# Retention and two feed-forward layers on one core: weight loads two pairs ahead, and the last chunk stored by halves

## The chip, the cores and the metric

The kernel runs on one core of a Trainium2 chip. The metric is the device time of one execution, in microseconds (us). TensorE (PE) multiplies matrices, PEld is its weight load, VectorE (DVE) and ScalarE (ACT) work elementwise, GpSimd (POOL) scales a few operands, and SyncE (SP) issues every DMA transfer of this kernel, in program order, on one queue.

## The reference, cut to what matters

```python
# B, H, S, D = 4, 8, 576, 64
scores = q @ k.T / sqrt(D)
ret = (scores * Dmat) @ v          # Dmat[h, i, j] = gamma[h]**(i - j) where i >= j, else 0
x = ret.transpose(0, 2, 1, 3).reshape(B * S, H * D)          # 2304 x 512
g = x @ w_gate;  x = (g * sigmoid(g) * (x @ w_val)) @ w_out  # inner size 1536
r = max(x @ w_in, 0);  out = (r * r) @ w_out2                # inner size 2048
```

q, k and v are 32-bit floats. The five weight matrices are 64-bit floats.

## The kernel before, in words

**Attention, the first 128 us.** There are 16 pairs, each a batch and two heads. The loop at L515 has one turn n per pair and two more, because the second half of a pair (`apply`) runs two turns late (LAG = 2). A turn issues `load_kv(n+1)` and `load_qk(n+2)` on SP, then on PE `scores(n)` for four row blocks, `apply(n-2)` into the bank `o`, `scores` for the fifth block, `states(n)` into the bank `kvs`, and the fifth block of `apply(n-2)`, which writes into the bank of `scores(n)` behind the columns that VectorE reads for `pl`. VectorE masks the scores into `p_sb` and `pl` and carries the state `sb`. ScalarE copies `o` into the activations `xy`, and scales the keys of the next pair in `prep_state` (`kv_sb<-kv_sb,ks_sb`). In turns 3 to 6 `split_x` splits a quarter of the first 512 tokens of `xy` into `xh` (fp32r) and the rest `xl`. From turn 6 on `hidden1_early` computes one gate or value block of the first token chunk in each turn, 12 matmuls of 128x512 in a bank `g` or `v`. qk_p has three buffers and kv_p four, so a load waits until the pair that held its buffer is done.

**Weights.** A unit is a 128x512 block of a weight matrix. `prefetch` loads it as 128x1024 words into `raw` (512 KB), from a pool of two buffers, or into a `spare` area. The generator `conversion` (L161) turns a unit into fp32 in five steps: ScalarE takes the low and the high words (`raw<-raw`, `w<-raw`), VectorE clamps, shifts, merges and adds (the add is the row `CUSTOM_DVE_ANT_0`, printed as `ISA` in the order of instructions). In the third step of the next unit `parts_unit` splits it into `w_hi` (ScalarE) and `w_lo` (VectorE). `pump` runs so many steps at given places of the loops. While the attention runs, every instruction is chained to the one before it on its engine, so the order in the code is the order on the engine.

The line that starts the conversion in turn 3 (FROM is 6) is

```python
            if n == FROM - 3:
                prefetch(1)
            if new:
                scores(n, range(NC - 1))
            pump(fill if n == FROM - 3 else 2 * fill)
```

and from there on a turn advances one unit. UNITS_EARLY = 15 units are meant to be converted in the attention. Their parts live in a pool of WA = 21 pairs of tiles.

**The seam and after.** After turn 17 `split_x` splits the second token chunk. Then come the steps of the first layer and of the second one: `hidden1` (24 matmuls) and `out1` (12 matmuls, into four banks `a`) for each of 12 blocks f, and `hidden2` and `out2` for 16 blocks, for five token chunks. Every product has three matmuls: hi by hi, hi by lo, lo by hi. Right behind the seam stand `hidden1` of chunk 1 and six `out1` of chunk 0 (the early blocks), which need the units 12 to 17. Behind the attention the order is not chained but left to a scheduler. The last chunk of the second layer has 256 tokens, two banks `a`; `out2` copies one with ScalarE and one with VectorE into `o_sb` and stores each with one transfer (L366 to L371).

Of the kernel before, what the change touches and what calls it, by code (L numbers as in the profile page):

```python
# [9 lines left out]
F32 = mybir.dt.float32  # L10
# [4 lines left out]
ALU = mybir.AluOpType  # L15
# [4 lines left out]
DM = H * D  # L20
NT = B * S
P = 128
CC = DM // P
F1 = 1536 // P
F2 = 2048 // P
NC = -(-S // P)
N = 512
CHUNKS = {
    1: [(0, 512), (512, 512), (1024, 256), (1280, 512), (1792, 512)],
    2: [(0, 512), (512, 512), (1280, 512), (1792, 512), (1024, 256)],  # L30
}
NCH = len(CHUNKS[1])
# [4 lines left out]
FROM = 6  # L37

LAG = 2

WA = 21

WARM = 4
UNITS_EARLY = WA - HALF

PUMPS = {0: 1, 1: 4, 2: 1}
# [9 lines left out]
def retention_moe_kernel(  # L56
# [56 lines left out]
    pe, dve, act, pool_e, sp = map(Chained, (nc.tensor, nc.vector, nc.scalar, nc.gpsimd, nc.sync))  # L113
# [6 lines left out]
    raw_t, raw_flat, w_t = {}, {}, {}  # L120
    spare = []
# [82 lines left out]
    def pump(k=1):  # L204
        for _ in range(k):
            if pumped["n"] < pumped["limit"]:
                pumped["n"] += 1
                next(convert, None)
# [144 lines left out]
    def out2(n, f):  # L353
        if f == 0:
            acc[2, n] = accs(CHUNKS[2][n][1] // P)
        h = hs.pop((2, n, f))
        ensure((2, "o", f))
        w = units[2, "o", f]
        for tt in range(CHUNKS[2][n][1] // P):
            three(acc[2, n][tt], cut(h, tt * P, P), w, f == 0, f == F2 - 1)  # L360
        if f == F2 - 1:
            for tt, a in enumerate(acc.pop((2, n))):
                if tt % 2 == 0:
                    o = raw_p.tile([P, 1024], U32, tag="raw", name="o_sb").bitcast(F32)
                t = o[:, (tt % 2) * 512:][:, :512]
                if tt % 2:  # L366
                    dve.tensor_copy(t, a)
                else:
                    act.copy(t, a)
                r0 = CHUNKS[2][n][0] + tt * P  # L370
                sp.dma_start(out=out[r0:r0 + P, :], in_=t)  # L371


# [2 lines left out]
    with ExitStack() as st:  # L376
        const = pool(st, "const", 1)
# [9 lines left out]
        rs = [slice(h * D, (h + 1) * D) for h in range(2)]  # L387
        pairs = [(b, hp) for b in range(B) for hp in range(NP)]

        def warm():  # L390

            one = const.tile([P, 256], F32, tag="one", name="one")
            dve.memset(one, 1.0)
            ps = bank("g")
            for _ in range(WARM):
                pe.matmul(ps[:, :256], one[:, :P], one, start=True, stop=True)

        def load_qk(n):
# [7 lines left out]
        def load_kv(n):  # L406
            b, hp = pairs[n]
            kv_t[n] = kv_p.tile([P, 2 * NC - 1, P], F32, tag="kv", name="kv_sb")
            sp.dma_start(out=kv_t[n], in_=kv[b, hp])
            if n < NP:  # L410
                sp.dma_start(out=mask_sb[:, n], in_=mask[:, n])
                sp.dma_start(out=qs_sb[:, n], in_=qscale[:, n, P:P + qs_sb.shape[-1]])

        def prep_state(n):
            hp = pairs[n][1]
            for h, r in enumerate(rs):
                kn = kv_t[n][:, NC:, r]
                act.mul(kn, kn, ks_sb[:, hp, 1, h])
            qs = q_p.tile([P, S - P], F32, tag="qs", name="qs")
            for c, m in ((0, 3 * P), (3 * P, D)):  # L420
                w = min(m, P)
                pool_e.tensor_tensor(
                    out=qs[:, c:c + m].rearrange("p (c q) -> p c q", q=w),
                    in0=qk_t[n][:, 0, P + c:P + c + m].rearrange("p (c q) -> p c q", q=w),
                    in1=qs_sb[:, hp, None, :w].to_broadcast([P, m // w, w]), op=ALU.mult,
                )
            q_t[n] = qs
# [73 lines left out]
            act.copy(xy[:, hp, t0:t0 + bank.shape[-1]], bank)  # L501

        chain["on"] = True
        warm()
        mask_sb = const.tile([P, NP, 2, P], F32, tag="mask", name="mask_sb")
        ks_sb = const.tile([P, NP, NC - 1, 2, 1], F32, tag="ks", name="ks_sb")

# [4 lines left out]
        prep_state(0)  # L512
        last = len(pairs) - 1
        pumped["limit"] = 5 * UNITS_EARLY
        for n in range(last + 1 + LAG):  # L515
            new, old, nxt = n <= last, n >= LAG, n + 1 <= last
            fill = PUMPS[0] if n >= FROM - 3 else 0
            if nxt:
                load_kv(n + 1)
            if n + 2 <= last:  # L520
                load_qk(n + 2)
            if n == FROM - 3:
                prefetch(1)
            if new:
                scores(n, range(NC - 1))
            pump(fill if n == FROM - 3 else 2 * fill)
            if old:
                apply(n - LAG, False)
            pump(fill)
            if LAG < n <= LAG + CC:  # L530
                split_x(1, 0, n - LAG - 1)
            if new:
                scores(n, (NC - 1,))
            pump(fill)
            if new:
                states(n)
            pump(fill)
            if FROM <= n < FROM + 2 * HALF:
                hidden1_early(n - FROM)
            if old:  # L540
                apply(n - LAG, True)
            if nxt:
                prep_state(n + 1)
        for cc in range(CC):
            split_x(1, 1, cc)
    chain["on"] = False


# [98 lines left out]
```

## Time and profile before

| | |
|---|---|
| median of three runs | 943.98 us (943.98 to 945.04) |
| the profiled execution's own time | 942.15 us |
| its span | 940.4 us |
| mean granted TensorE clock, as a share of 2.4 GHz | 0.991 |
| PE busy | 920.8 us (98%) |
| DVE, ACT, POOL busy | 466.3, 340.9, 21.3 us |
| HBM read, written | 56.44 MB, 5.77 MB |

The times of the parts below are those of the profiled execution, counted from the start of its span. A row of the timeline gives start, duration, engine, operation, output<-input and the number of merged instructions; what stands in brackets is the idle time before it and what ended that. All rows carry L106, a helper through which the engines are called, so they are told apart by their tiles.

### The profile page before, as it was taken

Reading aid. Unit: us, or ns where it says so; the run is one execution under the profiler, and the core shown is the slowest. Engines: PE = TensorE matmul, PEld = TensorE weight load, DVE = VectorE, ACT = ScalarE, POOL = GpSimd, SP = SyncE. Lnnn points to the kernel's source line nnn. Section 1 sums busy time; section 2 is a strip of 40 time slices with the busy share of each in tenths; the row PEclk is TensorE's granted clock in tenths of the full one; section 3 lists DMA queues with packets and bytes.
Section 4 is the critical chain, followed back from the end, with each engine's and each line's share of the span. In section 5 each row is a group of like instructions: output and inputs, shape, how many; then the busy total and the mean of one; then the engine's idle time right before and its main releaser. Section 6 shows DMA issues by size and latency. Waiting matters only on the chain.

```text
span 940.4 us, 12525 instructions
## 1 busy us (share of the span) xinstructions
PE 920.8 (98%) x5144; PEld 769.6 (82%) x5144; DVE 466.3 (50%) x845; ACT 340.9 (36%) x629; POOL 21.3 (2%) x39
## 2 busy tenths in 40 slices
PE   8699999999999999999999999999999999999998
PEld 6577778878889998888888888888888888888896
DVE  3688778797424242223899886242224223322332
ACT  2465565554312121112665664232223223222222
POOL 2111100000000000000000000000000000000000
PEclk8799999999999999999999999999999999999999
DMA  8676453542100000001244420000001000100000
GB/s 309 211 249 238 153 157 113 153 137 68 45 1 1 1 2 0 1 1 45 88 136 135 135 90 1 0 34 13 1 1 45 0 1 1 45 1 0 15 31 23
DMA packets 22024, 63.01 MB, mean 67 GB/s; under 512 B 2256, under 2 KB 3792, under 8 KB 21968
## 3 DMA queue, kind: packets, MB, share of 16 engines
q1 hardware_dynamic: 21968, 62.22, 19.6%
q8 instruction: 40, 0.66, 0.3%
q14 instruction: 16, 0.13, 0.0%
HBM read 56.44 MB, written 5.77 MB: 66 GB/s over the span
## 4 chain that ended last, share of the span: by engine, by line
PE 88%; DMA 5%; DVE 4%; ACT 2%; issue 1%; SPq 0%; ACTq 0%
PE a L106 33%; PE g L106 24%; PE v L106 24%; DMA raw<-in_w 3%; PE s L106 3%; PE o L106 3%; DVE w L106 2%; PE kvs L106 1%; DMA xy<-in_w 1%; DVE w_lo L106 1%; DVE t L106 1%; DMA kv_sb<-in_kv 0%; ACT raw L106 0%; DMA part<-part_sb 0%; DVE xl L106 0%
## 5 line engine op out<-in xcount | busy, mean ns | idle before, releaser
L106 ACT ACTIVATE t<-g 128x512 f32<-128x512 f32 (+1 forms) x100 | 55.4, 554 | 211.8 <-PE g L106 211.6
L106 ACT CAST h_hi<-t 128x512 fp32r<-128x512 f32 (+1 forms) x134 | 77.1, 575 | 119.2 <-DVE t L106 113.6
L106 DVE TENSOR_TENSOR h_lo<-t,h_hi 128x512 fp32r<-128x512 f32 (+1 forms) x134 | 85.2, 636 | 67.1 <-ACT h_hi L106 66.7
L106 PE MATMUL v<-xh,w_hi 128*128 128x512 f32 (+1 forms) x304 | 113.8, 374 | 0.0
L106 PE MATMUL g<-xh,w_hi 128*128 128x512 f32 (+1 forms) x304 | 113.8, 374 | 0.0
L106 PE MATMUL g<-xh,w_lo 128*128 128x512 f32 (+1 forms) x304 | 113.3, 373 | 0.0
L106 PE MATMUL v<-xh,w_lo 128*128 128x512 f32 (+1 forms) x304 | 113.2, 373 | 0.0
L106 PE MATMUL g<-xl,w_hi 128*128 128x512 f32 (+1 forms) x304 | 113.2, 372 | 0.0
L106 PE MATMUL v<-xl,w_hi 128*128 128x512 f32 (+1 forms) x304 | 113.2, 372 | 0.0
L106 PE MATMUL a<-w_lo,h_hi 128*128 128x512 f32 x288 | 112.3, 390 | 0.0
L106 PE MATMUL a<-w_hi,h_hi 128*128 128x512 f32 x288 | 112.2, 390 | 0.0
L106 PE MATMUL a<-w_hi,h_lo 128*128 128x512 f32 x288 | 110.1, 389 | 0.0
L106 DVE TENSOR_TENSOR t<-g,t 128x512 f32<-128x512 f32 (+1 forms) x60 | 38.2, 636 | 89.7 <-ACT t L106 89.6
L106 PE MATMUL a<-h_lo,w_hi 128*128 128x512 f32 (+1 forms) x216 | 79.0, 366 | 0.5 <-DVE h_lo L106 0.5
L106 PE MATMUL a<-h_hi,w_lo 128*128 128x512 f32 (+1 forms) x216 | 78.9, 366 | 0.0
L106 DVE SCALAR_TENSOR_TENSOR t<-g,t 128x512 f32<-128x512 f32 (+1 forms) x40 | 25.5, 639 | 105.6 <-ACT t L106 105.4
L106 PE MATMUL a<-h_hi,w_hi 128*128 128x512 f32 (+1 forms) x216 | 76.8, 367 | 0.1
L106 DVE SCALAR_TENSOR_TENSOR t<-v,t 128x512 f32<-128x512 f32 (+1 forms) x40 | 25.6, 639 | 91.7 <-ACT t L106 91.4
L106 DVE TENSOR_SCALAR w<-w 128x512 f32<-128x512 f32 (+1 forms) x136 | 57.4, 423 | 25.9 <-ACT w L106 24.4
L106 PEld LDWEIGHTS g<-xh,w_hi 128*128 128x128 f32 x304 | 57.3, 188 | 10.4 <-issue 0.2
L106 PEld LDWEIGHTS v<-xh,w_hi 128*128 128x128 f32 x304 | 57.3, 188 | 10.2 <-issue 0.2
L106 PEld LDWEIGHTS v<-xh,w_lo 128*128 128x128 f32 x304 | 57.3, 188 | 10.1
(81 smaller groups left out, 1477.6 us busy)
## 6 DMA issues: line engine op xcount, KB each, us to landing
raw<-in_w SPq DMA_DIRECT2D x51, 512.0 KB, 3.6
kv_sb<-in_kv SPq DMA_DIRECT2D x16, 576.0 KB, 4.0
xy<-in_w SPq DMA_DIRECT2D x17, 512.0 KB, 3.7
qk_sb<-in_qk SPq DMA_DIRECT2D x15, 576.0 KB, 5.1
out<-o_sb SPq DMA_DIRECT2D x18, 256.0 KB, 2.2
part<-part_sb SPq DMA_DIRECT2D x4, 256.0 KB, 2.9
xy<-part SPq DMA_DIRECT2D x1, 1024.0 KB, 5.2
mask_sb<-in_mask SPq DMA_DIRECT2D x4, 128.0 KB, 7.3
```

What stands on the lines that cost most here:

```text
L106: i = op(*args, **kw)
```

## The change

It changes six things.

- The first two weight loads are issued in turn 2 instead of 3 (`FROM - 4`), the conversion starts in turn 4 instead of 3 (`FROM - 2`), and a third load buffer, `raw3`, joins the two of the pool while the attention runs. 14 units instead of 15 are converted there (WA = 20). The loads of the loop stop at unit 13 and are all taken up when it ends: one more step of conversion is pumped, and the third buffer is given up.
- In turn 17 the fifth block of `apply` comes ahead of `hidden1_early`.
- The load of the first keys and values is cut in two, keys first, and one of the two scalings of these keys goes from ScalarE to VectorE.
- Of four warming matmuls at the start three stay there and two more stand behind the first scores.
- `out2` of the last chunk copies the left half of each bank with ScalarE and the right half with VectorE, and stores each half with a transfer of its own: four of 128 KB instead of two of 256 KB.
- WA being one less, the pool of the later weight tiles has one more pair.

```diff
--- before.py
+++ after.py
@@ -38,9 +38,9 @@
 
 LAG = 2
 
-WA = 21
-
-WARM = 4
+WA = 20
+
+WARM = 3
 UNITS_EARLY = WA - HALF
 
 PUMPS = {0: 1, 1: 4, 2: 1}
@@ -363,11 +363,17 @@
                 if tt % 2 == 0:
                     o = raw_p.tile([P, 1024], U32, tag="raw", name="o_sb").bitcast(F32)
                 t = o[:, (tt % 2) * 512:][:, :512]
+                r0 = CHUNKS[2][n][0] + tt * P
+                if n == NCH - 1:
+                    for x, copy in enumerate((act.copy, dve.tensor_copy)):
+                        at = slice(x * (DM // 2), (x + 1) * (DM // 2))
+                        copy(t[:, at], a[:, at])
+                        sp.dma_start(out=out[r0:r0 + P, at], in_=t[:, at])
+                    continue
                 if tt % 2:
                     dve.tensor_copy(t, a)
                 else:
                     act.copy(t, a)
-                r0 = CHUNKS[2][n][0] + tt * P
                 sp.dma_start(out=out[r0:r0 + P, :], in_=t)
 
 
@@ -387,12 +393,10 @@
         rs = [slice(h * D, (h + 1) * D) for h in range(2)]
         pairs = [(b, hp) for b in range(B) for hp in range(NP)]
 
-        def warm():
-
-            one = const.tile([P, 256], F32, tag="one", name="one")
-            dve.memset(one, 1.0)
+        def warm(k):
+
             ps = bank("g")
-            for _ in range(WARM):
+            for _ in range(k):
                 pe.matmul(ps[:, :256], one[:, :P], one, start=True, stop=True)
 
         def load_qk(n):
@@ -406,7 +410,8 @@
         def load_kv(n):
             b, hp = pairs[n]
             kv_t[n] = kv_p.tile([P, 2 * NC - 1, P], F32, tag="kv", name="kv_sb")
-            sp.dma_start(out=kv_t[n], in_=kv[b, hp])
+            for at in (slice(NC, 2 * NC - 1), slice(0, NC)) if n == 0 else (slice(0, 2 * NC - 1),):
+                sp.dma_start(out=kv_t[n][:, at], in_=kv[b, hp][:, at])
             if n < NP:
                 sp.dma_start(out=mask_sb[:, n], in_=mask[:, n])
                 sp.dma_start(out=qs_sb[:, n], in_=qscale[:, n, P:P + qs_sb.shape[-1]])
@@ -415,7 +420,10 @@
             hp = pairs[n][1]
             for h, r in enumerate(rs):
                 kn = kv_t[n][:, NC:, r]
-                act.mul(kn, kn, ks_sb[:, hp, 1, h])
+                if n or h:
+                    act.mul(kn, kn, ks_sb[:, hp, 1, h])
+                else:
+                    dve.tensor_scalar(out=kn, in0=kn, scalar1=ks_sb[:, hp, 1, h], scalar2=None, op0=ALU.mult)
             qs = q_p.tile([P, S - P], F32, tag="qs", name="qs")
             for c, m in ((0, 3 * P), (3 * P, D)):
                 w = min(m, P)
@@ -501,7 +509,9 @@
             act.copy(xy[:, hp, t0:t0 + bank.shape[-1]], bank)
 
         chain["on"] = True
-        warm()
+        one = const.tile([P, 256], F32, tag="one", name="one")
+        dve.memset(one, 1.0)
+        warm(WARM)
         mask_sb = const.tile([P, NP, 2, P], F32, tag="mask", name="mask_sb")
         ks_sb = const.tile([P, NP, NC - 1, 2, 1], F32, tag="ks", name="ks_sb")
 
@@ -512,18 +522,22 @@
         prep_state(0)
         last = len(pairs) - 1
         pumped["limit"] = 5 * UNITS_EARLY
+        loads["cap"], loads["open"] = UNITS_EARLY - 1, True
+        spare.append(const.tile([P, 2, 512], F32, tag="raw3", name="raw3"))
         for n in range(last + 1 + LAG):
             new, old, nxt = n <= last, n >= LAG, n + 1 <= last
-            fill = PUMPS[0] if n >= FROM - 3 else 0
+            fill = PUMPS[0] if n >= FROM - 2 else 0
             if nxt:
                 load_kv(n + 1)
             if n + 2 <= last:
                 load_qk(n + 2)
-            if n == FROM - 3:
+            if n == FROM - 4:
                 prefetch(1)
             if new:
                 scores(n, range(NC - 1))
-            pump(fill if n == FROM - 3 else 2 * fill)
+            if n == 0:
+                warm(2)
+            pump(fill if n == FROM - 2 else 2 * fill)
             if old:
                 apply(n - LAG, False)
             pump(fill)
@@ -535,14 +549,20 @@
             if new:
                 states(n)
             pump(fill)
+            if n == last + LAG:
+                apply(n - LAG, True)
             if FROM <= n < FROM + 2 * HALF:
                 hidden1_early(n - FROM)
-            if old:
+            if old and n < last + LAG:
                 apply(n - LAG, True)
             if nxt:
                 prep_state(n + 1)
         for cc in range(CC):
             split_x(1, 1, cc)
+        pump(PUMPS[0])
+        assert loads["next"] == UNITS_EARLY and not raw_t
+        loads["cap"], loads["open"] = 3 * F1 - 1, False
+        spare.clear()
     chain["on"] = False
 
 
```

**SP, the loads around turn 2 and 3.** Before, the two raw loads stand behind kv and qk of turn 3 (waits in brackets are the semaphores that the instruction waits for):

```order
L106 DMA qk_sb<-in_qk 128x1152 [waits DMAHW2_49,PE_49,Pool_49]
L106 DMA kv_sb<-in_kv 128x1152 [waits DMAHW3_49,PE_49,Activation_49]
L106 DMA qk_sb<-in_qk 128x1152 [waits DMAHW4_49,Pool_49]
L106 DMA raw<-in_w 128x1024 [waits DMAHW5_49]
L106 DMA raw<-in_w 128x1024 [waits DMAHW6_49]
L106 DMA kv_sb<-in_kv 128x1152 [waits DMAHW7_49,PE_49,Activation_49]
L106 DMA qk_sb<-in_qk 128x1152 [waits DMAHW0_49,Pool_49]
L106 DMA raw<-in_w 128x1024 [waits DMAHW1_49,DMAHW5_49,DVE_49,Activation_49]
```

Now:

```order
L106 DMA qk_sb<-in_qk 128x1152 [waits DMAHW3_49,PE_49,Pool_49]
L106 DMA raw<-in_w 128x1024 [waits DMAHW4_49]
L106 DMA raw<-in_w 128x1024 [waits DMAHW5_49]
L106 DMA kv_sb<-in_kv 128x1152 [waits DVE_49,DMAHW6_49,PE_49,Activation_49]
L106 DMA qk_sb<-in_qk 128x1152 [waits DMAHW7_49,Pool_49]
L106 DMA kv_sb<-in_kv 128x1152 [waits DMAHW0_49,PE_49,Activation_49]
L106 DMA qk_sb<-in_qk 128x1152 [waits DMAHW1_49,Pool_49]
L106 DMA raw_138<-in_w 128x1024 [waits DMAHW2_49]
```

The pair of raw loads has moved ahead of the kv and qk of turn 3; the third raw load stays in turn 4, but goes to the new buffer (raw_138) and no longer waits for a buffer to come free.

**DVE, turn 3 and the head of turn 4.** `p_sb` opens a turn, `xl` is the quarter that is split, `pl` is what PE waits for. Before:

```order
L106 TENSOR_TENSOR p_sb<-s,mask_sb 128x1024 [waits DMAHW0_49,PE_49]
L106 TENSOR_SCALAR w<-w 128x512 [waits Activation_49]
L106 TENSOR_TENSOR xl<-xy,xh 128x512 [waits Activation_49]
L106 TENSOR_TENSOR pl<-s,mask_sb 64x128 [waits PE_49]
L106 TENSOR_SCALAR w<-w 128x512 [waits DVE_49]
L106 SCALAR_TENSOR_TENSOR sb<-sb,qs_sb,kvs 128x64 [waits DMAHW1_49,Activation_49]
L106 SCALAR_TENSOR_TENSOR sb<-sb,qs_sb,kvs 128x64 [waits DVE_49] x2
L106 SCALAR_TENSOR_TENSOR w<-raw,w 128x512 [waits DMAHW5_49]
L106 TENSOR_TENSOR p_sb<-s,mask_sb 128x1024 [waits PE_49]
```

Now:

```order
L106 TENSOR_TENSOR p_sb<-s,mask_sb 128x1024 [waits DMAHW1_49,PE_49]
L106 TENSOR_TENSOR xl<-xy,xh 128x512 [waits Activation_49]
L106 TENSOR_TENSOR pl<-s,mask_sb 64x128 [waits PE_49]
L106 SCALAR_TENSOR_TENSOR sb<-sb,qs_sb,kvs 128x64 [waits DMAHW2_49,Activation_49]
L106 SCALAR_TENSOR_TENSOR sb<-sb,qs_sb,kvs 128x64 [waits DVE_49] x2
L106 TENSOR_TENSOR p_sb<-s,mask_sb 128x1024 [waits PE_49]
L106 TENSOR_SCALAR w<-w 128x512 [waits Activation_49]
L106 TENSOR_TENSOR xl<-xy,xh 128x512 [waits Activation_49]
L106 TENSOR_TENSOR pl<-s,mask_sb 64x128 [waits PE_49]
```

The first clamp of a weight unit, which waits for ScalarE, stood between `p_sb` and `xl` of turn 3; now it stands there in turn 4.

**PE, the end of turn 17.** `o` is the rest of the last `apply`, `s` its fifth block, `v` the last early block, `a` the first `out1` behind the seam. Before, the end of that stretch:

```order
L106 MATMUL v<-xh,w_lo 128x512
L106 MATMUL s<-qs,sb 64x64 x2
L106 MATMUL s<-pl,kv_sb 64x64 x2
L106 MATMUL a_1596<-w_hi 128x512
L106 MATMUL a_1596<-w_lo,w_hi 128x512
L106 MATMUL a_1596<-w_hi,w_lo 128x512
```

Now, its head:

```order
L106 MATMUL o<-p_sb,kv_sb 64x128 x8
L106 MATMUL s<-qs,sb 64x64 x2
L106 MATMUL s<-pl,kv_sb 64x64 x2
L106 MATMUL v<-xh,w_hi 128x512
L106 MATMUL v<-xl,w_hi 128x512
L106 MATMUL v<-xh,w_lo 128x512
L106 MATMUL v<-xh,w_hi 128x512
```

The two rows of `s` have moved from behind the 12 matmuls of `v` to ahead of them; `a` now follows `v` directly.

## Rows read from the trace of the kernel before

**Rows 1.** The page's slices: PE's busy share and granted clock in 40 slices.

```profile
PE   8699999999999999999999999999999999999998
...
PEclk8799999999999999999999999999999999999999
```

**Rows 2.** Waits of PE, whole span: engine, tile, releaser, us in total, times, longest.

```profile
PE s L106 <- DVE pl L106: 9.2, 3, 6.6
PE kvs L106 <- ACT kv_sb L106: 2.4, 1, 2.4
PE a L106 <- ACT xy L106: 1.5, 1, 1.5
...
PE a L106 <- DVE h_lo L106: 0.5, 1, 0.5
```

**Rows 3.** Timeline of turns 1 to 3: start, us, engine, operation.

```profile
11.62 0.33 SPq L106 DMA_DIRECT2D kv_sb<-in_kv  x1
...
20.05 0.91 ACT L106 ACTIVATE kv_sb<-kv_sb,ks_sb 128x256 f32<-128x256 f32 x2 [0.46 <-DMA kv_sb<-in_kv]
20.26 0.90 SPq L106 DMA_DIRECT2D raw<-in_w  x2
...
21.16 1.09 PE L106 MATMUL o<-p_sb,kv_sb 128*64 128x128 f32 x16
...
26.51 0.65 ACT L106 ACTIVATE raw<-raw 128x512 uint32<-128x512 uint16 x1 [5.56 <-DMA raw<-in_w]
...
29.34 0.27 DVE L106 TENSOR_TENSOR pl<-s,mask_sb 64x128 f32<-64x128 f32 x1
...
29.76 0.48 PE L106 MATMUL s<-qs,sb 64*64 64x64 f32 x4 [6.63 <-DVE pl L106]
```

**Rows 4.** Windows: busy us of PE, PEld, DVE, ACT, POOL, PEclk, DMA share, GB/s.

```profile
30.00:31.00 1.00, 1.00 (x12) 0.77 (x12) 0.93 (x4) 0.31 (x2) 0.63 (x1) 0.50 0.06 16
```

**Rows 5.** Timeline of turns 4 to 6.

```profile
38.25 0.33 PE L106 MATMUL s<-qs,sb 64*64 64x64 f32 x4 [1.20 <-DVE pl L106]
...
41.81 0.59 ACT L106 COPY xy<-o 128x512 f32<-128x512 f32 x1 [0.75 <-PE o L106]
...
43.98 0.33 PE L106 MATMUL s<-qs,sb 64*64 64x64 f32 x4 [1.34 <-DVE pl L106]
...
51.24 0.33 PE L106 MATMUL s<-qs,sb 64*64 64x64 f32 x4
```

**Rows 6.** Windows, as in rows 4, ten microseconds.

```profile
10.00:20.00 10.00, 10.00 (x134) 8.69 (x132) 5.44 (x13) 3.25 (x9) 2.30 (x5) 0.71 0.99 381
```

**Rows 7.** Timeline around the seam.

```profile
124.06 0.33 SPq L106 DMA_DIRECT2D raw<-in_w  x1
...
127.54 0.34 PE L106 MATMUL s<-pl,kv_sb 128*64 128x64 f32 x4
...
129.43 0.50 PE L106 MATMUL a<-w_hi 128*128 128x512 f32 x1 [1.55 <-ACT xy L106]
...
134.56 0.34 SPq L106 DMA_DIRECT2D raw<-in_w  x1
...
144.96 0.69 DVE L106 TENSOR_TENSOR w_lo<-w,w_hi 128x512 fp32r<-128x512 f32 x1
```

**Rows 8.** Chain that ended last, in order of time: start, us, what.

```profile
210.03 2.72 PE g L106 x12
```

**Rows 9.** Timeline of the end.

```profile
935.55 0.59 ACT L106 COPY o_sb<-a 128x512 f32<-128x512 f32 x1 [1.53 <-PE a L106]
935.78 0.69 DVE L106 COPY o_sb<-a 128x512 f32<-128x512 f32 x1 [1.30 <-PE a L106]
936.16 0.81 SPq L106 DMA_DIRECT2D out<-o_sb  x2
```

**Rows 10.** Groups of 128x256 that read PSUM, from 900 us: busy us, mean ns.

```profile
L106 ACT ACTIVATE t<-g 128x256 f32<-128x256 f32 x6 | 2.3, 385 | 8.1 <-PE g L106 8.1
...
L106 DVE SCALAR_TENSOR_TENSOR t<-g,t 128x256 f32<-128x256 f32 x6 | 2.5, 425 | 7.8 <-ACT t L106 7.7
```

## The prediction

> **What bounds the kernel now.** I read the page's slices first: PE is busy in nine tenths or more of nearly every slice, and its granted clock is full except in the first two [rows 1]. So the kernel is bound by its matmuls, and time can be won only where PE stands still or runs at half clock. The list of what PE waited for has those places [rows 2]: 9.2 us for `pl` in three waits, the longest 6.6; 2.4 us for the first scaled keys; 1.5 us for `xy`; 0.5 us for one `h_lo`. Everything else on DVE and ACT lies under matmuls.
>
> The 6.6 us are turn 3. SP issues the two raw loads at 20.26, behind the kv and qk of that turn, and ACT, whose next instruction is the first step of the conversion, starts it at 26.51, as soon as they have landed [rows 3]. Behind it in ACT's order stand the copy of `o` and `xh`; in DVE's order the clamp `w`, `xl` and `pl`. PE had finished `o` at 22.25 (21.16 + 1.09) and gets `pl` at 29.62 (29.34 + 0.28) [rows 3]. Then a second price: PE's clock is at 0.50 of 2.4 GHz, that is at 1.2 GHz, in the microsecond from 30 [rows 4], after that standstill. Turn 4 (from `s` at 29.76 to `s` at 38.25) takes 8.49 us, turn 5, at full clock and with the same instructions, 5.73 (38.25 to 43.98), turn 6 with its early block 7.26 [rows 3, 5].
>
> **The change, part by part.** The sum is made against the profiled execution, 942.15 us for a span of 940.4. It lies 1.83 us under the median of the runs, 943.98, so I take the difference off that median.
>
> *Earlier loads, later conversion.* In the new order turn 3 has no conversion on ACT or DVE, and the raw loads stand right behind the qk of turn 2. What then holds `s` of turn 3 is what holds it in turn 5: `o` ends, ACT copies it (41.81) and makes `xh`, DVE makes `xl` and `pl`, and `s` comes at 43.98, so 2.2 us after the end of `o` [rows 5]. From 22.25 that gives 24.4 instead of 29.76: 5.4 us won. Turn 4 now starts the conversion as turn 3 did, with loads that have long landed, and at full clock should take turn 5's 5.73 instead of 8.49: 2.76 won. Turns 5 and 6 keep their lengths. Together **8.1 us**; the same from the ends: 24.4 + 2 x 5.73 = 35.9 where 43.98 stood.
>
> Is there room on the queue? DMA is at a share of 0.99 from 10 to 20 us and moves 381 GB/s [rows 6]. The two loads are 1.05 MB, which at that rate is 2.75 us. The bytes up to the qk of turn 3 don't change in number, only in order: before they had all landed by 26.5, when ACT's wait ended. In the new order the queue has no lull around 20 us, so they land about 25, the raw pair ahead of kv and qk of turn 3. These keys are scaled at the head of turn 4 and first read by `states` late in it, some 3 us later. Cost 0; bounds 0 and 2.75 us (rival 2). The third buffer and the unit that moves a turn later cost nothing: a unit's parts are finished in the turn ahead of the one whose early block reads them, and from turn 6 on PE fills the turn.
>
> *Start.* Cutting the first keys and values in two, one scaling on DVE and the two moved warming matmuls can shorten PE's 2.4 us wait for the first scaled keys [rows 2]. But the next keys come by DMA: kv of pair 3, issued at 11.62, is scaled at 20.05, the instant it lands [rows 3], with the queue full [rows 6]. What is won at 9 us waits again at 20. I take 0, bounds -1.2 us (half of that wait) and 0.
>
> *The fifth block ahead of the last early block.* PE ends `s` at 127.88 (127.54 + 0.34) and starts `a` at 129.43, because ACT's copy of that `s` frees the bank only then [rows 7]. In the new order 12 matmuls of `v` (2.72 us per 12 [rows 8]) stand between, the copy is done under them, and `a` follows at once: **1.5 us** won; bounds 0 and 1.55.
>
> *One unit less at the seam.* At the seam units 12 and 13 are loaded, 14 is under way as unit 15 was before (issued at 124.06), and unit 15 must wait for 14's buffer. Before, a buffer turned from 124.06 to 134.56, in 10.5 us; and from its load at 134.56 a unit (17) needed till 145.65 (144.96 + 0.69), 11.1 us, to be split [rows 7]. All in the clock of before: in the new order unit 17 is loaded two turns after 124.06, so it is split at 124.06 + 21.0 + 11.1 = 156.2 at the latest. PE reads it after 113 further matmuls (60 of `a`, the 24 of `hidden1` and 29 that the scheduler has pulled forward), 25.6 us at 0.2267 each [rows 8], so at 127.9 + 25.6 = 153.5. At that pace PE would stand 2.7 us. But the splits of the second chunk and a wait for two other loads lie in that turn of 10.5 us; worked through instruction by instruction I get about 8 us for each turn and nothing lost. I take 0, bounds 0 and 2.7. Units 18 to 35 are needed later still: PE stood 0.5 us for one `h_lo` in that stretch [rows 2], and in the new order each of these `h_lo` stands behind one to three units fewer. 0, bounds -0.5 and +1.
>
> *Store by halves.* Before, ACT copies one bank from 935.55 and DVE the other from 935.78 till 936.47; the two stores are issued from 936.16 on, in 0.81 us [rows 9]. For 256 columns the nearest rows are 385 ns on ACT and 425 on DVE [rows 10]. DVE's half of a bank waits for ACT's half in the new program: 935.55 + 0.385 + 0.425 = 936.36, and the second bank's 936.79, 0.3 later than before. SP issues four stores at 0.4 each from 935.94 on, the last near 937.1 instead of 936.56; it carries half as many bytes. I take +0.2, bounds -0.3 and +0.6. The Trainium skill ("PSUM — Partial Sum Buffer", section "Terms") says that no two engines may access the same bank within the same partition in one cycle; by that rule the halves of a bank gain nothing from two engines. No row of this kernel shows two engines on one bank; the +0.3 above is that wait, and without it the sum would be 0.3 lower.
>
> Sum: -8.1 + 0 - 1.5 + 0 + 0.2 = **-9.4 us**, so 934.6; I say 934.5.
>
> **Rivals.**
> 1. *The weights run dry at the seam (slower).* If a buffer's turn there grows, because 15 waits for 14 and 17 for 15 while the second chunk's splits sit in ACT's and DVE's order between, PE stands at the first `out1` blocks. The gain of 9.4 is gone when unit 17 is ready at 153.5 + 9.4 = 162.9, a turn of (162.9 - 11.1 - 124.06) / 2 = 13.9 us. At 16 us a turn it is ready at 167.2: 13.7 lost, 948. For it: one load alone is under way at the seam, and the next waits for it. Against: the turn before was 10.5 with more in it. 4%.
> 2. *The wait moves to kv.* If loads in flight share the engines evenly, the raw pair pushes kv of pair 3 back by up to 2.75 us, from 20.05 to 22.8. ACT scales till 23.7, copies `o` behind it, and `s` comes near 26.0 instead of 24.4: 936.1. For it: kv took 8.4 us from its issue at 11.62. Against: it was issued ahead of the pair. The Trainium skill ("DMA: Bandwidth & Descriptors", "Queues, rings and completion order") says that an engine consumes the descriptors of a ring in ring order; by it kv would not be pushed back and this rival would be void. The 8.4 us do not decide that. 18%.
> 3. *The clock falls all the same.* PE still stands some 1.3 us per turn in turns 3 to 5, and waits for kv. If the grant drops to 1.2 GHz again, turn 4 keeps its 8.49 us: 937.3. Against: PE stood 1.20 us at 38.25 and went on at full clock [rows 5]. 14%.
> 4. *The conversions bind later.* They run from the seam to 208 without much rest, and one unit more is left to them; if that unit's 5.25 us (half of 10.5) all shows at an `h_lo`, and the 1.5 of the seam with it, 941.3. 6%.
> 5. *The loads do not start earlier*, since SP is in order and each transfer waits for the eighth before it (raw 0 for kv of pair 2). Then the turn without conversion still helps, and rival 2's time is its bound. Counted there.
>
> **How the numbers follow.** Forecast 58%, rivals 2, 3, 4, 1 as above. Low end: the forecast less 1.2 and 1.3 for start, seam and store, 932.0, and 0.5 for the scatter of runs: 931.5. High end: rivals 2 and 3 together, 934.5 + 1.6 + 2.76 = 938.9, so 939. Outside stay rivals 1 and 4 and some of the low side, a fifth at most. Runs can tell about 0.2%, 1.9 us. Rivals 2 and 3 and nearly all of 4 are faster by more than that; rival 1 is spread over no change and slower, and I keep as much again for what I have not seen: faster 0.91, same 0.04, slower 0.05.
>
> **What would show it.** Right: the 6.6 us wait for `pl` is gone, `s` of turn 3 near 24.4, of turn 5 near 35.9, clock full from 26 to 36, raw landed before ACT asks, `a` right behind `v`. Wrong: ACT waiting for kv_sb beyond 21 us, PE at half clock in turn 4, or new PE waits for `w_hi` or `w_lo` behind the seam.

## The result and the profile after

The changed kernel takes 935.25 us (median of four runs, 934.69 to 936.49), where the kernel before took 943.98 on the same chip: 8.7 us less by the medians; the ratio is 0.9912 (95% interval 0.9892 to 0.9931), which is 8.3 us. The forecast was 934.5, with a range of 931.5 to 939.0. The profiled execution took 934.81 us for a span of 933.0, so it is 7.34 us shorter than that of before (942.15) and its span 7.4.

The list of PE's waits, after (engine, tile, releaser, us in total, times, longest), answers to [rows 2]:

```profile
PE s L106 <- DVE pl L106: 5.1, 3, 2.4
PE s L106 <- DMA qk_sb<-in_qk: 1.9, 2, 1.3
PE g L106 <- DVE one L106: 1.2, 1, 1.2
PE a L106 <- DVE h_lo L106: 0.6, 2, 0.4
PE a L106 <- ACT h_hi L106: 0.5, 1, 0.5
```

The wait of 6.6 us for `pl` is gone, and so are those for the first scaled keys and for `xy`. Small waits have come in for qk and `h_hi`; the one for `h_lo` was 0.5 and is 0.6. The wait for `one` was there before, with the same 1.2 us. The window from 30 to 31 us, in which the clock stood at 0.50 [rows 4], reads now (same columns)

```profile
30.00:31.00 1.00, 0.00 (x0) 0.00 (x0) 0.81 (x2) 0.27 (x2) 0.00 (x0) 1.00 1.00 367
```

The clock is at 1.00, that is 2.4 GHz, but PE stands in this very microsecond. The timeline of turns 2 to 5 shows why (start, us, engine, operation):

```profile
12.56 0.33 SPq L106 DMA_DIRECT2D kv_sb<-in_kv  x1
...
16.09 0.80 SPq L106 DMA_DIRECT2D raw<-in_w  x2
...
18.57 0.33 PE L106 MATMUL s<-qs,sb 64*64 64x64 f32 x4
...
19.25 0.33 SPq L106 DMA_DIRECT2D kv_sb<-in_kv  x1
...
21.10 0.91 ACT L106 ACTIVATE kv_sb<-kv_sb,ks_sb 128x256 f32<-128x256 f32 x2 [1.67 <-DMA kv_sb<-in_kv]
...
24.30 0.33 PE L106 MATMUL s<-qs,sb 64*64 64x64 f32 x4 [1.34 <-DVE pl L106]
...
27.15 0.91 ACT L106 ACTIVATE kv_sb<-kv_sb,ks_sb 128x256 f32<-128x256 f32 x2 [2.00 <-DMA kv_sb<-in_kv]
...
27.96 0.66 ACT L106 ACTIVATE raw<-raw 128x512 uint32<-128x512 uint16 x1
...
28.52 0.65 ACT L106 ACTIVATE w<-raw 128x512 f32<-128x512 f32 x1
...
29.07 0.56 ACT L106 COPY xy<-o 128x512 f32<-128x512 f32 x1
...
31.22 0.33 PE L106 MATMUL s<-qs,sb 64*64 64x64 f32 x4 [2.43 <-DVE pl L106]
...
36.95 0.33 PE L106 MATMUL s<-qs,sb 64*64 64x64 f32 x4 [1.34 <-DVE pl L106]
```

Turn 3 ends as forecast (`s` at 24.30). In turn 4 ScalarE waits 2.00 us for the keys of pair 4, which land at 27.15. Behind that wait stand, in its order, the two steps of the conversion and the copy of `o`; so `pl` comes late, and the turn takes 6.92 us instead of 5.73.

At the seam and at the end:

```profile
120.48 0.39 PE L106 MATMUL v<-xh,w_lo 128*128 128x512 f32 x1
120.71 0.39 PE L106 MATMUL a<-w_hi 128*128 128x512 f32 x1
...
928.15 0.65 ACT L106 COPY o_sb<-a 128x256 f32<-128x256 f32 x2 [1.53 <-PE a L106]
928.54 1.79 SPq L106 DMA_DIRECT2D out<-o_sb  x4
928.55 0.76 DVE L106 COPY o_sb<-a 128x256 f32<-128x256 f32 x2 [1.48 <-ACT o_sb L106]
```

`a` follows `v` without a gap, where it waited 1.55 us [rows 7]. VectorE's half of a bank waits for ScalarE's, and four issues take 1.79 us where two took 0.81 [rows 9]; the span ends 4.85 us after the first copy begins, as before (940.4 - 935.55).

Six points of each profile cut the time into stretches: `s` of the fifth block in turns 2 to 5, the first `a` behind the seam, the first copy of the last results (us). The kernels below the first two rows are those of the experiments; for the last four (v1, z1, z2, z3) the text gives the points that it uses.

| kernel | s 2 | s 3 | s 4 | s 5 | first a | first copy |
|---|---|---|---|---|---|---|
| before | 18.73 | 29.76 | 38.25 | 43.98 | 129.43 | 935.55 |
| changed | 18.57 | 24.30 | 31.22 | 36.95 | 120.71 | 928.15 |
| changed, again (y0) | 20.11 | 25.83 | 31.56 | 37.29 | 121.04 | 927.67 |
| loads in turn 3 (x1) | 17.93 | 23.66 | 29.39 | 35.12 | 118.90 | 924.36 |
| loads in turn 1 (x6) | 20.17 | 25.90 | 31.63 | 38.91 | 122.66 | 929.70 |
| before, early loads (x2) | 18.09 | 26.41 | 34.28 | 40.01 | 125.32 | 930.92 |
| before, late conversion (x5) | 18.86 | 24.59 | 31.88 | 37.61 | 123.12 | 930.38 |
| seam order back (x3) | 18.11 | 23.84 | 29.96 | 35.70 | 121.15 | 927.74 |
| start back (y1) | 17.90 | 23.63 | 30.24 | 37.52 | 121.26 | 928.85 |
| whole stores (y3) | 18.29 | 24.02 | 29.75 | 35.48 | 119.26 | 925.78 |

From the first two rows the 7.4 us come apart, stretch by stretch: to `s` of turn 2 -0.16; turn 3 -5.30; turn 4 -1.57; turn 5 0; from there to the first `a` -1.69; from `a` to the first copy +1.32; the end 0. Together -7.40.

### The profile page after: what moved, and what is told of

The parts are those of the page before. It is cut to its first block, busy times and chain, and to the rows that moved or that the text cites. A ratio compares the mean times of both kernels' runs of the same rounds, so it can differ in the third digit from the quotient of the medians.

```text
span 933.0 us, 12533 instructions
## 1 busy us (share of the span) xinstructions
PE 918.8 (98%) x5146; PEld 766.9 (82%) x5146; DVE 465.5 (50%) x851; ACT 339.6 (36%) x629; POOL 20.6 (2%) x39
## 4 chain that ended last, share of the span: by engine, by line
PE 84%; DMA 8%; DVE 4%; ACT 3%; issue 1%; SPq 0%; DVEq 0%; ACTq 0%
PE a L106 32%; PE g L106 23%; PE v L106 23%; DMA raw<-in_w 4%; PE o L106 3%; PE s L106 2%; DVE w L106 2%; DMA xy<-in_w 2%; DMA kv_sb<-in_kv 1%; DMA qk_sb<-in_qk 1%; ACT raw L106 1%; PE kvs L106 1%; DVE t L106 1%; ACT w L106 1%; DVE w_lo L106 1%
## 5 line engine op out<-in xcount | busy, mean ns | idle before, releaser
L106 DVE SCALAR_TENSOR_TENSOR t<-v,t 128x512 f32<-128x512 f32 (+1 forms) x40 | 25.6, 639 | 92.1 <-ACT t L106 91.7
L106 PEld LDWEIGHTS g<-xl,w_hi 128*128 128x128 f32 x304 | 57.3, 188 | 10.4 <-DVE xl L106 0.5
```

Of the source, the lines that this page charges most:

```text
L106: i = op(*args, **kw)
```

## The experiments

Each ratio is that of a kernel to the kernel before on the same chip, with its 95% interval; for the changed kernel it was 0.9912 and, in y0, 0.9898. Each profile is one execution.

**The two halves of the main term, each alone.** x2 is the kernel before with

```diff
-            if n == FROM - 3:
+            if n == FROM - 4:
                 prefetch(1)
```

> The kernel before with the first two raw loads issued in turn 2 instead of 3, and nothing else. Theory: the transfers end about 2.5 us earlier, ScalarE begins the conversion near 24 instead of 26.51, s of turn 3 comes near 27.2 instead of 29.76, and with PE's standstill shorter the clock may stay full: s of turn 5 between 38.7 (turn 4 at 5.73, and 5.73) and 41.4 instead of 43.98, so 2.6 to 5.3 us faster than before. Rival: the loads were never what counted, the conversion's place is; then s of turn 3 comes within 0.5 us of 29.76.

Measured: 938.58 us, ratio 0.9954 (0.9940 to 0.9968). ScalarE begins the conversion at 23.16, `s` of turn 3 comes at 26.41 and of turn 5 at 40.01, 4.0 us earlier: the theory, but for the clock, which was at half from 24.4 to 31.3. What ScalarE waits for is still the raw words, and PE behind it still stands:

```profile
23.16 0.65 ACT L106 ACTIVATE raw<-raw 128x512 uint32<-128x512 uint16 x1 [3.18 <-DMA raw<-in_w]
```

x5 is the kernel before with

```diff
-            fill = PUMPS[0] if n >= FROM - 3 else 0
+            fill = PUMPS[0] if n >= FROM - 2 else 0
-            pump(fill if n == FROM - 3 else 2 * fill)
+            pump(fill if n == FROM - 2 else 2 * fill)
```

> The kernel before with the conversion starting in turn 4 instead of 3, and nothing else: the loads stay in turn 3, two buffers, order at the seam, start and stores as before. Theory (the early loads are not needed once the conversion is late): s of turn 3 at 24.4, raw lands near 26.5 as before and is converted ahead of the copy of o, s of turn 4 near 30.1, s of turn 5 near 35.9; 8 us faster than before by the attention alone, less what one unit fewer at the seam may cost there (0 to 2.7). Rival: with two buffers and loads in turn 3 turn 4 still waits, s of turn 5 beyond 38.

Measured: 935.65 us, ratio 0.9918 (0.9904 to 0.9933). `s` of turn 3 is where it should be (24.59), without early loads and without a third buffer. Turn 4 takes 7.29 us instead of 5.73, and not by a longer wait: PE stands 1.34 us there as in turn 5, but its clock is at half from 25.6 to 29, and the same matmuls take longer (the row of `s` takes 1.16 us at full clock):

```profile
24.59 0.33 PE L106 MATMUL s<-qs,sb 64*64 64x64 f32 x4 [1.34 <-DVE pl L106]
...
25.12 1.67 PE L106 MATMUL s<-qk_sb 64*128 64x128 f32 x16
26.72 1.54 PE L106 MATMUL o<-qs,sb 64*64 64x128 f32 x12
28.20 1.47 PE L106 MATMUL o<-p_sb,kv_sb 128*64 128x128 f32 x16
...
31.88 0.33 PE L106 MATMUL s<-qs,sb 64*64 64x64 f32 x4 [1.34 <-DVE pl L106]
```

So the later conversion alone brings 7.0 us and the early loads alone 4.0, by the medians, where the whole change brings 8.7 and, in y0, 9.6; the two don't add.

**Where the pair of loads stands on the queue.** x1 is the changed kernel with the pair back in turn 3, x6 with the pair in turn 1; y0 is the changed kernel once more. The order of PE, DVE and ACT is the same in all.

```diff
-            if n == FROM - 4:
+            if n == FROM - 3:
                 prefetch(1)
```

> The changed kernel with its pair of first raw loads issued in turn 3, behind kv and qk of that turn, as before; nothing else moves. In the changed kernel turn 4 took 6.92 us (24.30 to 31.22) where 5.73 was forecast, and ScalarE waited 2.00 us, till 27.15, for the keys of pair 4. Theory: the early raw pair pushes these keys back on the queue. Then the keys land about 2.75 us earlier here (the pair's bytes at 381 GB/s), near 24.4, raw lands near 27, the copy of o starts near 28.2 instead of 29.07, s of turn 4 comes near 30.4 and s of turn 5 near 36.1 instead of 36.95: 0.8 us faster than the changed kernel. Rival: the conversion's two steps in front of the copy of o cost the 1.2 us wherever the loads stand; then s of turn 5 stays at 36.95 or comes later.

Measured: 933.69 us, ratio 0.9903 (0.9887 to 0.9919). The keys of pair 4 are scaled at 24.41 with no wait, the raw words land at 25.86, and turn 4 takes 5.73:

```profile
19.48 1.03 SPq L106 DMA_DIRECT2D raw<-in_w  x2
...
24.41 0.91 ACT L106 ACTIVATE kv_sb<-kv_sb,ks_sb 128x256 f32<-128x256 f32 x2
25.86 0.69 ACT L106 ACTIVATE raw<-raw 128x512 uint32<-128x512 uint16 x1 [0.54 <-DMA raw<-in_w]
...
29.39 0.33 PE L106 MATMUL s<-qs,sb 64*64 64x64 f32 x4 [1.34 <-DVE pl L106]
```

The expected change came about, and more (`s` of turn 5 at 35.12, 1.8 earlier, 0.6 of it at the start). The total can't be told from the changed kernel's: the intervals lie over one another.

> The changed kernel with the first two raw loads one turn earlier still, in turn 1, ahead of kv and qk of pair 3. Theory (the pair pushes back whatever stands behind it on the queue): the keys of pair 3, scaled at 21.10 in the changed kernel, land about 2.75 us later, ScalarE copies o behind them, s of turn 3 comes near 26 instead of 24.30, and turn 4 gets back the 1.2 it lost: s of turn 5 near 37.5, so 0.5 slower than the changed kernel. Rival (order on the queue costs nothing): s of turns 3 and 5 within 0.6 us of the changed kernel's.

```diff
-            if n == FROM - 4:
+            if n == FROM - 5:
                 prefetch(1)
```

Measured: 936.38 us, ratio 0.9929 (0.9914 to 0.9944), against 0.9898 for the changed kernel on that chip. The keys of pair 3 are pushed back, to 22.57 (21.10 in the changed kernel), but turn 3 still takes 5.73: the copy of `o` was not yet due. `s` of turn 3 comes at 25.90, near the 26 expected, but not for the reason given: PE was late already at `s` of turn 2, at 20.17, and y0, with the pair in turn 2, is as late there (20.11, below). On that chip x6 is 2.9 us slower than the changed kernel; its profile shows 1.55 of it, turn 5 at 7.28 us with the clock at half from 32.3 to 35.7. That the place of the pair is the cause is not shown.

> The changed kernel once more, unchanged, beside the three below on the same chip: its scatter is what their differences are read against. If the 2.00 us wait for the keys of pair 4 and the 2.7 us of small stops behind the seam belong to the kernel, they come again within 0.5 us; if they are the luck of one execution's transfers, they differ (the stops behind the seam were 0.7 to 2.7 us in the kernels so far).

Measured: 933.65 us, ratio 0.9898 (0.9883 to 0.9912). The same program gives another picture: PE is at half clock from 11.7 to 18.5, `s` of turn 2 comes 1.54 later, and then turn 4 has no wait for keys:

```profile
20.11 0.33 PE L106 MATMUL s<-qs,sb 64*64 64x64 f32 x4
...
20.79 0.33 SPq L106 DMA_DIRECT2D kv_sb<-in_kv  x1
...
26.59 0.91 ACT L106 ACTIVATE kv_sb<-kv_sb,ks_sb 128x256 f32<-128x256 f32 x2
...
31.56 0.33 PE L106 MATMUL s<-qs,sb 64*64 64x64 f32 x4 [1.34 <-DVE pl L106]
```

By `s` of turn 5 the two executions are 0.34 us apart. So the size of that wait belongs to one execution. With the pair of raw loads in turn 2, ScalarE gets the keys of pair 4 at 27.15 (changed), 26.89 (v1), 26.17 (y1), 25.87 (x3) and 25.62 (y3), after waits of 2.00, 1.76, 1.68, 1.17 and 0.75 us, and in y0 at 26.59 without one; turn 4 takes 6.92, 6.69, 6.61, 6.12, 5.73 and 5.73. In x1, x5 and z1, with the pair in turn 3, it never waits for them. y3 loses nothing in turn 4, though its PE is earlier at `s` of turn 2 (18.29) than the changed kernel's (18.57):

```profile
25.62 0.91 ACT L106 ACTIVATE kv_sb<-kv_sb,ks_sb 128x256 f32<-128x256 f32 x2 [0.75 <-DMA kv_sb<-in_kv]
```

So it isn't only whether PE is early or late; the landing of these keys itself differs by 1.5 us from one execution to another.

**The seam.** x3 is the changed kernel with the fifth block behind the early block again:

```diff
-            if n == last + LAG:
-                apply(n - LAG, True)
             if FROM <= n < FROM + 2 * HALF:
                 hidden1_early(n - FROM)
-            if old and n < last + LAG:
+            if old:
                 apply(n - LAG, True)
```

> The changed kernel with the fifth block of the last pair behind the last early block again, as before. At the seam the first a should wait 1.5 us for the copy of s again. In the changed kernel PE stands 2.75 us in small stops between the seam and 233, before 1.48. Theory A: these stops come from the one unit fewer at the seam or from the order there, not from PE's being early; they stay, and the kernel is 1.5 us slower than the changed one. Theory B: the conversions bind there, so what PE gains at the seam it gives back at the stops between 170 and 233; here they shrink by about as much, and the kernel is slower by 0.5 us or less.

Measured: 935.93 us, ratio 0.9928 (0.9912 to 0.9943). The wait is back:

```profile
121.15 0.50 PE L106 MATMUL a<-w_hi 128*128 128x512 f32 x1 [1.51 <-ACT xy L106]
```

From `s` of turn 5 to `a` it takes 85.45 us, as before, and 83.74 to 83.78 in the six kernels of the table with the new order: 1.7 us. The total, 1.5 to 2.8 us above the changed kernel's by the two ratios, speaks for theory A, but does not show it: the intervals of x3 and of the changed kernel lie over one another, and x3's profiled execution (934.39) was no longer than the changed kernel's (934.81). The stops themselves (between the matmuls from 100 to 300 us, what a start comes later than 0.2267 us behind the one before) don't decide it: 2.1 us here, but 1.0 to 3.3 in those six, which have one and the same order there.

> The changed kernel with one weight unit fewer again converted in the attention (13, a pool of 19 pairs). Open is whether the unit that the change leaves to the time behind the seam costs anything there: PE's small stops between the seam and 300 us were 1.9, 1.4 and 2.9 us in three kernels with 15 units (the last one another order in the attention) and 1.0 to 3.3 in seven with 14, five of them between 2.2 and 3.1. Theory A (a unit less costs half a us or so, as forecast at 0 with bounds 0 and 2.7): the stops here stay under 3.5 us and the total within 1.5 us of the changed kernel's ratio to before, 0.990 to 0.991. Theory B (the units at the seam are just in time): the second unit fewer makes a new wait for w_hi, h_hi or h_lo of 2 us or more behind the seam, and the kernel is 2 us or more slower than the changed one.

```diff
-WA = 20
+WA = 19
```

Measured: 937.91 us, ratio 0.9946 (0.9932 to 0.9960), 3 to 4.5 us slower than the changed kernel: theory B, though the wait is for another tile than those named. Not all of it stands at the seam: its profile has 1.5 us in turn 5, which takes 7.24 us with the clock at half from 32.7 to 36.1. From `s` of turn 5 (38.21) to the first copy (932.05) it takes 893.84 us, against 889.24 to 891.33 in the six kernels of the table with the new order and 14 units, so 2.5 us at least come behind turn 5.

```profile
124.13 0.50 PE L106 MATMUL g<-xh,w_hi 128*128 128x512 f32 x1 [2.02 <-ACT xh L106]
...
125.83 0.79 PE L106 MATMUL g<-xl,w_hi 128*128 128x512 f32 x1 [0.17 <-DVE xl L106]
```

and, as windows (columns as in [rows 4]),

```profile
122.00:124.00 2.00, 0.11 (x1) 0.00 (x0) 1.57 (x4) 2.00 (x5) 0.00 (x0) 1.00 0.65 231
124.00:128.00 4.00, 3.69 (x9) 2.48 (x10) 4.00 (x7) 3.15 (x7) 0.00 (x0) 0.60 0.11 15
```

In the changed kernel the first `a` products, which need unit 12, stand from 120.71 on and cover ScalarE's splits of the second chunk:

```profile
122.25 2.18 ACT L106 CAST xh<-xy 128x512 fp32r<-128x512 f32 x4
...
123.43 0.39 PE L106 MATMUL g<-xh,w_hi 128*128 128x512 f32 x1
```

In v1 the first `a` comes at 129.79. With that unit unfinished nothing stands in front of them, PE stops for 2.0 us, and the four microseconds behind it run at a mean clock of 0.60. One unit fewer was free of a wait at the seam; the second was not.

**Start and stores.** y1 takes the four edits of the start back, y3 the stores by halves.

```diff
-WARM = 3
+WARM = 4
...
-            if n == 0:
-                warm(2)
...
-            for at in (slice(NC, 2 * NC - 1), slice(0, NC)) if n == 0 else (slice(0, 2 * NC - 1),):
+            for at in (slice(0, 2 * NC - 1),):
...
-                if n or h:
-                    act.mul(kn, kn, ks_sb[:, hp, 1, h])
-                else:
-                    dve.tensor_scalar(out=kn, in0=kn, scalar1=ks_sb[:, hp, 1, h], scalar2=None, op0=ALU.mult)
+                act.mul(kn, kn, ks_sb[:, hp, 1, h])
```

> The changed kernel with its start as before: four warming matmuls in front, none behind the first scores, first keys and values in one transfer, both scalings on ScalarE. Theory (the prediction): worth 0, s of turn 2 within 0.6 us of 18.57 because the transfers set it, and the total within 1 us of the changed kernel. Rival: in the changed kernel the clock was full from 7 to 40 us, with the start of before it was at half from 9 to 15.5 and, with the late conversion alone, again from 25.8 to 29; the moved warming matmuls keep it. Then here the clock is at half from 9 to 15 and again for some 3 us near 26, turn 4 takes 1.5 us longer, and the kernel is 1.5 to 2.5 us slower than the changed one.

Measured: 934.24 us, ratio 0.9903 (0.9887 to 0.9920); 0.6 us over y0, within the scatter. `s` of turn 2 comes at 17.90, as early as any and 0.67 from the 18.57 of the changed kernel. The clock is at half from 10.5 to 14.0 and from 31.0 to 34.4, and turn 5 takes 7.28: of the rival the two falls of the clock came, but not the price in the total. What it says of the changed kernel, a full clock from 7 to 40 us, is a misreading (last section), and falls came with the new start too: early in y0, in turn 5 of x6 and v1. The start is worth nothing that these runs can tell; whether it bears on the clock stays open.

```diff
-                if n == NCH - 1:
-                    for x, copy in enumerate((act.copy, dve.tensor_copy)):
...
-                    continue
```

> The changed kernel with the last chunk's results copied and stored as before, one bank each by ScalarE and VectorE, two transfers of 256 KB. Theory: the halves win nothing, since VectorE waits for ScalarE's half of the same bank and four issues take 1.8 us; from the start of the first copy to the end of the span both need 4.85 us, here too, within 0.3. Rival: the smaller last transfer is worth it, and here the tail takes 5.2 or more.

Measured: 934.26 us, ratio 0.9900 (0.9885 to 0.9915). From the first copy to the end of the span 4.72 us (930.5 - 925.78), against 4.85 and 4.83 in the two profiles with halves. The halves win nothing.

**What is left in turns 3 to 5.** PE waits 1.34 us in each for `pl`, which stands behind `xl` on VectorE. z1 (from x1), z2 (from the changed kernel) and z3 (from the kernel before) make `pl` first:

```diff
-            if LAG < n <= LAG + CC:
-                split_x(1, 0, n - LAG - 1)
             if new:
                 scores(n, (NC - 1,))
+            if LAG < n <= LAG + CC:
+                split_x(1, 0, n - LAG - 1)
```

> The kernel of x1 (the changed kernel with the raw pair in turn 3) with the split of a quarter behind the fifth block's scores in the code instead of ahead of them, so that VectorE makes pl before xl; the products on PE stay in their order. What is left between turns 3 and 5 are three waits of 1.34 us for pl, which stands behind xl on VectorE. Theory: PE was held there by VectorE's order alone; the waits fall to 0.3 or less, s of turn 5 comes near 32.3 instead of 35.12, and the kernel gains 2.8 us on x1. Rival: the queue is the bound in these turns (DMA at a share of 0.9 and more from 8 to 30 us); then the wait moves to the keys or to qk, s of turn 5 comes within 1 us of 35.12, and the total is that of x1.

> The same move in the changed kernel itself, with the raw pair in turn 2. Theory of the pushed keys: PE is earlier at turns 3 and 4 while the keys of pair 4 land when they did (25.6 to 27.2), so here the wait for them grows and s of turn 5 comes 1 to 2 us later than in the kernel with the pair in turn 3. Rival: the place of the pair makes no difference, both give the same s of turn 5 within 0.6 us.

> The kernel before with that move alone. Turn 3 there is held by the conversion, whose clamp stands ahead of pl on VectorE as well, and by the raw words that land at 26.5; so pl comes near 28.2 instead of 29.34, and turns 4 and 5 lose their waits of 1.20 and 1.34. Expected: s of turn 5 near 40.3 instead of 43.98, 3 to 4 us faster than before if the clock is as before. Rival: the clock, at half from 26 on, sets these turns, and 1 us or less is won.

Measured: z1 931.57 us, ratio 0.9896 (0.9880 to 0.9913); z2 931.73, 0.9897 (0.9882 to 0.9912); z3 940.59, 0.9986 (0.9977 to 0.9996). In z2 turn 3 takes 4.33 us instead of 5.73, and what it won waits in turn 4 for the same keys:

```profile
22.85 0.33 PE L106 MATMUL s<-qs,sb 64*64 64x64 f32 x4
...
26.58 0.91 ACT L106 ACTIVATE kv_sb<-kv_sb,ks_sb 128x256 f32<-128x256 f32 x2 [2.88 <-DMA kv_sb<-in_kv]
...
29.40 0.33 PE L106 MATMUL s<-qs,sb 64*64 64x64 f32 x4 [1.18 <-DVE pl L106]
```

`s` of turn 5 comes at 34.64 in z1 and 35.15 in z2, within the 0.6 us that the rival of z2 named. But z1's execution was late at the start (`s` of turn 2 at 19.52, with the clock at half from 11.0 to 17.8) and z2's was not (18.52): from `s` of turn 2 to `s` of turn 5 it takes 15.12 us in z1, 16.63 in z2 and 17.19 in x1. So what the place of the pair is worth there is not told by these two profiles. Of the 2.8 us that z1 was to gain on x1, 2.07 came in these turns, 1.41 of it in turn 3, and the late start hid most of it. What is left in z1 are waits for `pl`, not for the keys or qk, as its rival had it; the one in turn 4 stands behind ScalarE's wait for the raw words, and the 1.36 of turn 5 behind the conversion's add and clamp, which stand ahead of `pl` on VectorE.

```profile
26.86 0.67 ACT L106 ACTIVATE raw<-raw 128x512 uint32<-128x512 uint16 x1 [1.36 <-DMA raw<-in_w]
...
28.88 0.33 PE L106 MATMUL s<-qs,sb 64*64 64x64 f32 x4 [0.65 <-DVE pl L106]
```

z3 won 1.3 us by its ratio where 3 to 4 were expected, and its `s` of turn 5 came at 41.60 instead of 40.3; its conversion still holds turn 3 (PE waits 5.33 us for `pl`), and the clock is at half from 27.4 to 34.3. z1 and z2 have the lowest medians of all, on a chip where the kernel before was the fastest too (941.55); their ratios lie level with y0's 0.9898, so neither is shown to beat the changed kernel.

## Why the prediction was right, point by point

*Earlier loads, later conversion: -8.1 forecast, -6.9 in the first profile (turn 3 -5.30, turn 4 -1.57), -8.1 in the second (-5.31 and -2.76).* The mechanism is the one forecast: `s` of turn 3 came at 24.30, where 24.4 was the sign named. `s` of turn 5 came at 36.95 instead of 35.9, and a sign of being wrong came too, ACT waiting for `kv_sb` beyond 21 us, till 21.10 and then till 27.15. What failed is the sentence that the keys of pair 4, behind the raw pair, cost nothing because `states` reads them late. They did land later (at 27.15, and in x1, with the pair behind them, by 24.41), and it is not `states` that pays: ScalarE works in order, and behind its wait for them stood the conversion and the copy of `o`. That cost 1.2 us in the first profile and from 0 to 1.0 in the five others with this order. It is rival 2, one turn later than I placed it: I pushed back the keys of pair 3, which were issued ahead of the pair (12.56) and landed 8.54 us after their issue, 8.43 before [rows 3]. The Trainium skill ("DMA: Bandwidth & Descriptors", "Queues, rings and completion order") has the descriptors of a ring consumed in ring order; these rows agree, and in x6, with the pair ahead of these keys, they need 9.44 (13.13 to 22.57). Single profiles differ, though: in x3, also with the pair behind them, they needed 7.02 (12.10 to 19.12).

*Rival 5 did not come, and would have cost nothing.* The loads did start earlier (16.09 instead of 20.26). I had bounded the case that they don't by rival 2's 936.1, 1.6 us over the forecast. x5 shows that late conversion with loads in their old place is worth 7 us, and x1 that the old place serves the changed kernel as well, as far as the runs tell. So the early loads, half of the term as I gave it, were not needed; the conversion's place counts most.

*Rival 3, the clock.* It did not fall in turn 4 of the changed kernel, but it did in x5, and in turn 5 of y1, x6 and v1, at about 1.5 us each time, where I had priced it at 2.76. That PE once stood 1.20 us at full clock was no proof.

*Start: 0 forecast, -0.16 measured*, and y1 agrees: `s` of turn 2 lies between 17.9 and 18.9 in the five profiles with the old start, and between 17.9 and 20.2 in the nine with the new one.

*Seam: -1.5 forecast, -1.7 measured* at that place; that all of it reaches the total is not shown. Most of the rest is the first product behind the standstill: 0.33 us from its start to the next one (129.43 to 129.76), where the pace is 0.23.

*One unit less and the late stretch: 0 forecast with bounds; +1.32 in the first profile and +0.51 in the second.* From `a` to the first copy the kernels with 15 units took 806.12 (before), 805.60 (x2) and 807.25 us (z3), those with 14 from 805.46 to 807.59. Single profiles don't tell 14 units from 15. PE never waited for `w_hi` or `w_lo`, so rival 1 did not come; v1 shows how near it was, since one more unit less costs 2.5 us or more behind turn 5, with a wait of 2.0 us for `xh`.

*Stores: +0.2 forecast, 0 measured.* Four issues take 1.0 us longer than two, and the end comes neither sooner nor later. The banks are never read by two engines at once in this program, so the rule on banks that the prediction weighed is not tried by any run.

The total came out near because the parts that missed were small, and in part by luck: against the sum of -9.4 the span of the first profile fell by 7.4, since turn 4 lacked 1.2 us and the late stretch 1.3; the spread of executions is of that size (y0: -7.9 in the span).

## What to carry to other kernels

A load that is moved ahead on a full queue can push back what stands behind it, as it did here in five profiles of six; look up which engine waits for that, and what stands behind the wait in its order, before its cost is put at nothing. Where work waits for a transfer, ask first whether the work can come later: here that alone brought 7.0 of the 8.7 us, with no buffer more. And where one engine is early in one execution and late in the next, compare the stretches of two profiles of the same program before a difference of 1 us is given a cause.

## What the runs showed of the hardware

Two executions of one program differ in the clock at the start. In y0 it was at 0.50 (1.2 GHz) from 11.7 to 18.5, after PE had waited 1.66 us for qk. In the first profile of the changed kernel the clock column reads 1.00 from 7 to 40 us, but its trace has no record of the clock before 12.9 us, and the matmuls tell otherwise: these four took 2.07 us, where the same four took 1.13 in y0 (from 6.67).

```profile
7.74 2.07 PE L106 MATMUL g<-one 128*128 128x256 f32 x4
```

So both executions had a slow stretch, one ahead of 12.9 us and the other behind 11.7. `s` of turn 2 came 1.54 us later in y0, and by `s` of turn 5 0.34 of it was left, since its turn 4 had no wait for keys. A clock column is read beside the durations of like matmuls. And the clock fell after much shorter stops than the 6.6 us of before: in x5 it fell at 25.6, behind a wait of 1.34 us, which in the changed kernel left it at 1.00. What tells these two apart stays open.
